# Another written-out order for the pieces of a linear-attention and channel-mix kernel

## The chip, the cores and the metric

The kernel runs on one core of a Trainium2 chip. The metric is the time of one execution on the device in microseconds (us). The core has a matrix engine (TensorE, PE in the profile, with its weight loads listed apart as PEld), a vector engine (DVE), a scalar engine (ACT), GpSimd (POOL, which here issues the loads), and SyncE (SP, which issues stores and a few copies). Each engine executes its own instructions strictly in program order and waits on semaphores for the others.

## The reference

Eight batches, eight heads of 64, 576 positions. First a linear attention without softmax, whose rows are normalised; then a channel mix in which each position is blended with the one before it.

```python
kv  = einsum('bhsd,bhse->bhde', k, v)            # per head 64 x 64
out = einsum('bhsd,bhde->bhse', q, kv)
x   = out / sqrt(mean(out*out, -1) + 1e-6) * g_norm   # -> (8, 576, 512)
x_prev = x shifted down by one position (zeros first)
xk = mu_k*x + (1-mu_k)*x_prev ;  xr = mu_r*x + (1-mu_r)*x_prev
kk = relu(xk @ w_k)                              # 512 -> 1024
v2 = (kk*kk) @ w_v                               # 1024 -> 512
y  = sigmoid(xr @ w_r) * v2                      # (8, 576, 512) float32
```

## The kernel before

Everything is kept transposed, channels on partitions, in bf16. The attention works batch by batch (b = 0 to 7); heads lie in pairs, and two pairs form a half z (0 or 1). Batches 0 and 1 are loaded and worked in halves, the others whole (the names then end in `.01`). The channel mix works in nine groups g of 512 positions, which run across batches; `xk` and `xr` are rings that hold four batches. A group needs the blended x of every batch that it touches.

The program is cut into named pieces. `Plan.add` records each with the engines it may run on, and `Plan.emit` goes through the string `ORDER` word by word and issues the instructions of each piece; `@A` or `@D` behind a name chooses ACT or DVE where both are possible. Since no scheduler comes after it, `ORDER` fixes the order on every engine's queue and on the queues of transfers. The order between engines is left to semaphores. Two readers of one PSUM tile on different engines run in the order in which they are written.

The pieces, with the line of their instructions in the profile:

| piece | engine | line | what it does |
|---|---|---|---|
| `ldh.k`, `ldh.v` | SP | L236 | fp32 load of half 0 of k, v of batch 0 into the space of `xk` |
| `cst` | ACT or DVE | L128, L130 | casts these to bf16 |
| `ld.q/k/v b`, `ld.wk/wr/wv` | POOL | L221, L226, L252 | loads with cast to bf16 |
| `seta`, `setp`, `setb`, `ident`, `perm`, `table` | DVE, POOL, ACT | L164 to L189, L144 | constants, first activation table |
| `small`, `tr9`, `cols` | SP, PE, DVE | L193, L211, L200 | mu and g as columns |
| `zz`, `z:512` | PE | L450 | matmuls of zeros, filler ahead of the first `k0` piece |
| `kv`, `kc`, `ks`, `kd` | PE, ACT or DVE, PE, ACT or DVE | L265, L128/L130, L271 | kv, copy, regrouping matmul, copy |
| `tq` | DVE | L358 | transposes q, two pieces a batch or half |
| `u` | PE | L282 | q times kv, 32-row tiles, two pieces a batch or half |
| `sq` | ACT | L379 | squares of u |
| `uc` | ACT or DVE | L134, L136 | g times u out of PSUM (not for batch 0) |
| `ss`, `rs` | PE, ACT | L408 (b 0, 1) or L388, L288 | sums of squares, reciprocal root |
| `sp` | SP | L430 | spreads `rs` over the partitions (from batch 2) |
| `mul`, `d` | DVE | L401, L405, L300 | normalised x, difference to its neighbour |
| `mk`, `mr`, `xk`, `xr` | ACT or DVE, DVE | L134, L136, L313, L320 | blends |
| `k`, `relu`, `ksq` | PE, ACT, DVE | L482, L507, L465, L493, L522 | first product, relu, square |
| `r`, `sig` | PE, ACT | L534, L544 | second product, sigmoid |
| `v`, `out`, `st` | PE, DVE, SP | L554, L567, L581, L456 | third product, gate, store |

A name's numbers are batch or group, then part: `kv2.01` is kv of batch 2, `k5.2` the third block of 128 rows of w_k in group 5, `u4.01.1` the second half of the positions of batch 4.

Loads: POOL issues them in the order of the `ld` words, each on one of eight semaphores in turn, so that the ninth waits for the first to land; a load also waits until its buffer (three each for k, v and q) is no longer read. PSUM is four tiles of two banks (`ps`), taken by kv, u, ss and the three products in the order in which they are written. `sigmoid` and the reciprocal root lie in different activation tables, so that ACT loads a table (L144) wherever a `sig` follows an `rs` or the other way round.

## Time and profile before

| what | us |
|---|---|
| three runs | 199.5, 200.09, 200.31 (median 200.09) |
| the profiled execution, its time | 200.13 |
| its span, first to last instruction | 198.4 |
| last matmul ends | 194.4 |
| first `kv` (kv0.0) starts | 7.29 |
| first `k0` piece starts | 17.01 |
| kv2.01, kv3.01, kv5.01 start | 40.67, 49.77, 58.89 |
| last load lands | 98.6 |

The table is read so: the span is what the profile sees of an execution, and 1.7 us of its time lie outside it. The granted TensorE clock is 0.997 of full speed in the mean. In the list of groups a row gives engine, operation and tile, the busy time, the mean of one instruction, and what ended the idle time before it; in a timeline a bracket gives the idle time ahead of an instruction and the releaser. "issue" as a releaser means that the profile shows no wait.

### The profile page before, as it was taken

The numbers are of one execution on the slowest core, as the hardware profiler recorded it, in microseconds if no ns is written. First come the engines' busy times: TensorE is split into PE (matmuls) and PEld (weight loads), VectorE is DVE, ScalarE is ACT, GpSimd is POOL, SyncE is SP. The second block draws the span as 40 slices with busy tenths as digits, with TensorE's granted clock in tenths as the row PEclk, the third lists the DMA queues.
The fourth block names the chain that finished last, engine by engine and source line by source line (L and its number), as shares of the span: only waits on it lengthen the run. The fifth ranks groups of instructions, "written<-read, shape, count | busy, mean of one in ns | idle before, by whom it ended". The sixth has DMA issues, their size and how long they took to land.

```text
span 198.4 us, 4225 instructions
## 1 busy us (share of the span) xinstructions
PE 188.4 (95%) x1735; PEld 93.3 (47%) x1760; DVE 137.8 (69%) x235; ACT 121.8 (61%) x158; POOL 23.7 (12%) x42
## 2 busy tenths in 40 slices
PE   7889989999999999999999999999999999999992
PEld 2445844443544544444358644444444444444451
DVE  2669998897959968998968497899659421520641
ACT  3365499949976689945778986882219840433410
POOL 7743442141313010000000000000000000000000
PEclk9999999999999999999999999999999999999998
DMA  6999999999999999999703511743213000310444
GB/s 223 191 202 214 204 201 207 214 206 216 206 235 264 216 235 272 260 240 256 210 3 88 175 72 56 220 112 78 45 47 111 2 3 0 140 71 0 153 167 160
DMA packets 21032, 30.63 MB, mean 154 GB/s; under 512 B 1932, under 2 KB 14484, under 8 KB 21012
## 3 DMA queue, kind: packets, MB, share of 16 engines
q0 software_dynamic: 11280, 16.19, 45.7%
q1 hardware_dynamic: 9588, 14.03, 22.2%
q8 instruction: 14, 0.23, 0.4%
q10 hardware_dynamic: 144, 0.13, 0.2%
q14 instruction: 6, 0.05, 0.1%
HBM read 33.56 MB, written 9.44 MB: 217 GB/s over the span
## 4 chain that ended last, share of the span: by engine, by line
PE 68%; DMA 26%; POOL 2%; issue 2%; DVE 0%; POOLq 0%
PE ps L554 27%; PE ps L507 24%; DMA v<-in_v_dram 19%; PE ps L534 12%; DMA w_v<-in_moe_w_v_dram 7%; PE ps L282 2%; PE ps L265 1%; PE ps L388 1%; POOL w_k L252 1%; POOL q L221 1%; PE ps L271 0%; POOL k L226 0%; POOL perm L189 0%; POOL v L226 0%; DVE out L581 0%
## 5 line engine op out<-in xcount | busy, mean ns | idle before, releaser
L554 PE MATMUL ps<-w_v,sqk 128*128 128x512 bf16 (+1 forms) x286 | 65.7, 373 | 0.9 <-issue 0.6
L507 PE MATMUL ps<-xk,w_k 128*128 128x512 bf16 (+1 forms) x280 | 58.1, 355 | 1.1 <-issue 0.8
L465 ACT ACTIVATE relu<-ps 128x1024 bf16<-128x1024 f32 x36 | 36.5, 1026 | 32.5 <-PE ps L507 28.8
L554 PEld LDWEIGHTS <-sqk 128*128 128x128 bf16 x296 | 27.8, 98 | 32.2 <-issue 2.5
L507 PEld LDWEIGHTS <-w_k 128*128 128x128 bf16 x288 | 27.5, 98 | 26.7 <-issue 1.4
L567 DVE TENSOR_TENSOR out<-ps,sig 128x1024 f32<-128x1024 f32 x16 | 19.4, 1221 | 21.9 <-PE ps L554 12.5
L534 PE MATMUL ps<-w_r,xr 128*128 128x512 bf16 x139 | 33.6, 379 | 0.3
L522 DVE TENSOR_TENSOR sqk<-relu 128x1024 bf16<-128x1024 bf16 x32 | 21.2, 684 | 10.0 <-ACT relu L465 9.7
L544 ACT ACTIVATE sig<-ps 128x1024 bf16<-128x1024 f32 x18 | 18.2, 1024 | 12.4 <-PE ps L534 11.5
L534 PEld LDWEIGHTS <-xr 128*128 128x128 bf16 x144 | 13.9, 98 | 16.3 <-issue 0.5
L379 ACT ACTIVATE sq<-ps 128x576 bf16<-128x576 f32 x32 | 19.9, 652 | 1.8 <-PE ps L282 1.5
L358 DVE STREAM_TRANSPOSE qT<-q 128x576 f32<-128x576 f32 (+1 forms) x20 | 14.7, 760 | 2.4 <-DMA q<-in_q_dram 2.3
L144 ACT ACT_TABLE_LOAD x12 | 15.4, 1283 | 0.9 <-PEq L607 0.7
L136 DVE TENSOR_SCALAR uT<-ps,cols 128x576 bf16<-128x576 f32 x13 | 10.4, 816 | 7.7 <-ACT sq L379 5.5
L136 DVE TENSOR_SCALAR md<-d,cols 128x576 bf16<-128x576 bf16 x44 | 13.8, 365 | 0.4
L134 ACT ACTIVATE uT<-ps,cols 128x576 bf16<-128x576 f32 x15 | 10.9, 742 | 2.9 <-PE ps L282 2.9
L300 DVE TENSOR_TENSOR d<-xT 128x1152 bf16<-128x1152 bf16 (+1 forms) x18 | 12.3, 689 | 0.4
L313 DVE TENSOR_TENSOR xr<-md,xT 128x1152 bf16<-128x1152 bf16 x14 | 10.4, 750 | 1.6 <-ACT md L134 1.4
L405 DVE TENSOR_TENSOR xT<-uT,rs 128x1152 bf16<-128x1152 bf16 x14 | 10.4, 750 | 1.1 <-ACT rs L288 0.6
L313 DVE TENSOR_TENSOR xk<-md,xT 128x1152 bf16<-128x1152 bf16 x14 | 10.4, 754 | 0.6 <-ACT md L134 0.4
L450 PE MATMUL ps<-zero 128*128 128x512 bf16 x28 | 9.4, 481 | 1.5 <-DVE zero L164 1.2
L282 PE MATMUL ps<-qT,kv 32*64 32x288 bf16 x256 | 8.5, 290 | 0.8 <-DVE qT L358 0.8
(53 smaller groups left out, 120.9 us busy)
## 6 DMA issues: line engine op xcount, KB each, us to landing
out_dram<-out SPq DMA_DIRECT2D x35, 256.0 KB, 2.3
v<-in_v_dram POOLq DMA_DIRECT2D x6, 576.0 KB, 22.9
k<-in_k_dram POOLq DMA_DIRECT2D x6, 576.0 KB, 23.2
q<-in_q_dram POOLq DMA_DIRECT2D x6, 576.0 KB, 25.5
rs<-rsc SPq DMA_DIRECT2D x48, 72.0 KB, 3.2
q<-in_q_dram POOLq DMA_DIRECT2D x4, 288.0 KB, 10.3
w_k<-in_moe_w_k_dram POOLq DMA_DIRECT2D x2, 512.0 KB, 11.4
w_v<-in_moe_w_v_dram POOLq DMA_DIRECT2D x2, 512.0 KB, 13.8
```

The costliest lines, as they stand in the source:

```text
L136: nc.vector.tensor_scalar(out=dst, in0=src, scalar1=col, scalar2=None, op0=ALU.mult)
L144: nc.scalar.preload_act_table_set(name)
L313: nc.vector.tensor_tensor(out=dst[:, 2 * z:2 * z + 2, r0:r0 + w], in0=md.t[:, :, cs], in1=xT[:, :, cur], op=ALU.add)
L358: nc.vector.transpose(out=dst[part, js], in_=src[part, js])
L379: sq_ = add("sq" + name, "A", lambda _, ps=ps, sq=sq, cs=cs, w=w: nc.scalar.activation(out=get(sq)[:, :, cs], in_=ps.t[:, :, 0:w], func=AF ...
L465: nc.scalar.activation(out=get(rt), in_=ps.t, func=AF.Relu)
L507: nc.tensor.matmul(get(ps)[:, fc % 2, a0:a1], w_k_sb[:, cc, 128 * fc:128 * fc + 128], xk[:, cc, x0:x0 + a1 - a0], start=(cc == 0), stop=(c ...
L522: nc.vector.tensor_mul(out=get(sqk)[:, 2 * f2:2 * f2 + 2, :], in0=rt.t, in1=rt.t)
L534: nc.tensor.matmul(get(ps)[:, ci % 2, :], xr[:, cc, n0:n0 + 128], w_r_sb[:, cc, :], start=(cc == 0), stop=(cc == NHP - 1))
L544: nc.scalar.activation(out=get(sg), in_=ps.t, func=AF.Sigmoid)
L554: nc.tensor.matmul(get(ps)[:, bank, cs], sqk.t[:, fc, 128 * ci:128 * ci + 128], w_v_sb[:, fc, cs], start=(fc == 0), stop=(fc == NFC - 1))
L567: dv = add(f"out{g}.{c2}", "D", lambda _, ps=ps, sg=sg, ot=ot: nc.vector.tensor_mul(out=get(ot), in0=ps.t, in1=sg.t), deps=ms + [sg_done], ...
```

## The change

Only the string `ORDER` changes. No piece is added or dropped but one `z:512` (30 words instead of 29), and no tile, size or dependency changes; what moves is the place of nearly every piece in the queues, and the engine of some copies.

- Loads: `ldh.v` goes ahead of `ldh.k` and `ident` ahead of the first load; `ld.k1.1` goes ahead of `ld.wk0`, `ld.v1.1` ahead of `ld.wk1`, `ld.k1.0` and `ld.v1.0` ahead of `ld.wr`; k and v of several batches swap, `ld.q5` and `ld.q6` and the loads of batches 6 and 7 swap.
- Engines: `kd` runs on DVE five times instead of once, `kc` once instead of twice, `cst` three times instead of twice, `uc` 14 times instead of 13; `mr` runs on ACT eight times instead of four. The words need two more table loads on ACT, 14 instead of 12.
- Startup: the pieces of batch 0 and 1 and of groups 0 and 1 are interleaved otherwise; kv0.1 goes ahead of u0.0.1, kd0.0 behind tq0.0.0.
- Middle: kv5.01, kv4.01, kv6.01 and kv7.01 stand elsewhere among the pieces of the channel mix, kv6.01 directly ahead of u5.01.0, kv7.01 ahead of u6.01.1, ss5 behind u6.01.0 and ss6 behind u7.01.0.
- End: the last piece is `v8.3.10` with its store on SP, where it was `v8.3.11` with its store on ACT.

The string is one line in the file; it is wrapped here and cut to the places that the prediction speaks of.

```diff
-ldh.k ldh.v seta setp perm ld.q0.0 ld.q0.1 ld.v0.1 ld.k0.1 ld.wk0 ident ld.wk1 ld.v1.1 ld.k1.1 ld.q1.1 ld.wr ld.q1.0 ld.v1.0 ld.k1.0 ld.wv0 ld.wv1
-ld.v2.01 ld.k2.01 ld.q2.01 table small zz cst.k0@D cst.k1@A setb cst.v0@A cst.v1@D tq0.0.1 tq0.0.0 z:512 z:512 z:512 z:512 z:512 z:512 z:512 z:512
-z:512 z:512 z:512 z:512 z:512 z:512 z:512 z:512 kv0.0 tq0.1.0 kc0.0@A z:512 z:512 ks0.0 tr9 cols kd0.0@A u0.0.0 sq0.00 z:512 z:512 z:512 ss0.00 u0.0.1
-rs0.00 mul0.00 d0.00 tq0.1.1 z:512 z:512 kv0.1 ld.k3.01 ld.v3.01 ld.q3.01 sq0.01 kc0.1@A ss0.01 rs0.01 ks0.1 kd0.1@A z:512 z:512 z:512 u0.1.0 sq0.10
-xk0.00 z:512 z:512 z:512 ss0.10 mul0.01 d0.01 xk0.01 rs0.10 mul0.10 d0.10 u0.1.1 k0.000 sq0.11 ss0.11 rs0.11 k0.110 xk0.10 k0.100 mul0.11 k0.001 d0.11
-xk0.11 relu0.00 xr0.11 xr0.00 k0.010 k0.011 kv1.1 ksq0.00 k0.111 kc1.1@A tq1.1.0 tq1.1.1 ks1.1 xr0.10 relu0.01 kd1.1@A relu0.11 ksq0.11 k0.101 xr0.01
-u1.1.1 uc1.11@A sq1.11 u1.1.0 sq1.10 uc1.10@D relu0.10 ksq0.10 r0.0 r0.1 ss1.2 ss1.3 rs1.2 rs1.3 mul1.1 kv1.0 ld.k5.01 ld.v5.01 kc1.0@D tq1.0.1
-tq1.0.0 r0.2 r0.3 sig0.0 ks1.0 kd1.0@A ksq0.01 sig0.1 v0.0.0 u1.0.1 uc1.01@D u1.0.0 v0.1.0 sq1.00 sq1.01 uc1.00@D v0.1.1 d1.1 ss1.1 rs1.1 v0.0.1
-out0.0 ss1.0 rs1.0 v0.2.0 v0.2.1 mul1.0 d1.0 mk1.0@D xk1.0 v0.3.0 v0.3.1 out0.1 mk1.1@A kv2.01
...
-u2.01.1 sq2.11 mr1.0@D k1.1.1 uc2.01@D k1.6.0 k1.7.0 k1.6.1 relu1.0 uc2.11@D u2.01.0 sq2.01 sq2.10 sq2.00 uc2.10@D k1.7.1 k1.4.0 k1.5.0 xr1.1 k1.4.1
-uc2.00@A ss2 kv3.01
...
-u3.01.0 sq3.00 v1.2.0 uc3.00@D v1.3.0 v1.2.1 sq3.10 u3.01.1 uc3.11@A uc3.10@D kv5.01 ld.k6.01 ld.v6.01 sq3.11 kc5.01@A v1.3.1 v1.1.0 ks5.01
...
-kv4.01 kc4.01@A k2.1 ks4.01 relu2.1 kd4.01@A st1.0 xr2.0 mr2.1@D xr2.1 ksq2.1 relu2.0 tq4.01.0 tq4.01.1 ld.q7.01 k2.4 k2.5 relu2.2 k2.6 r2.2 r2.3
-u4.01.0
...
-kv6.01 out3.0 kc6.01@A st2.3 xk4.0 xr4.0 ss5 rs5 sp5.0 v3.3.1 out3.1 ks6.01 st3.1 k4.6 kd6.01@A k4.7 relu4.3 u6.01.0
...
-kv7.01 mr5.1@A ss6 v4.2.0 mk5.0@D xk5.0 xk5.1 kc7.01@A ks7.01 out4.0 kd7.01@D st4.0 v4.2.1 xr5.1 rs6 sp6.1 u7.01.1 uc7.01@A uc7.11@A v4.3.1 sq7.11
-out4.1 st4.3 st2.0 st4.2 sq7.01 k5.2 k5.3
...
-rs7 v5.1.0 v5.2.0 v5.2.1 r5.2 v5.3.0 mk6.0@D mr6.1@D xk6.0 xr6.1 mr6.0@D r5.0 xr6.0 r5.1 sig5.0 r5.3 sig5.1 xk6.1 v5.0.0 sp7.1 v5.0.1 mul7.1 v5.3.1
-out5.1 r6.0 r6.1 k6.4
...
-v8.0.00 v8.1.10 sig8.0 st7.0 v8.2.00 v8.2.10 out8.10 st8.10 sig8.1 out8.20 st8.20 v8.0.10 out8.00 v8.3.00 v8.3.10 out8.30 st8.00 st8.30 v8.3.01
-v8.3.11 out8.31 st8.31
...
+ldh.v ldh.k seta table setp perm ident ld.q0.0 ld.q0.1 ld.v0.1 ld.k0.1 ld.k1.1 ld.wk0 ld.v1.1 ld.wk1 ld.q1.1 ld.k1.0 ld.v1.0 ld.wr ld.q1.0 ld.wv0
+ld.wv1 ld.k2.01 ld.v2.01 ld.q2.01 small zz cst.v0@D cst.v1@D cst.k0@A setb cst.k1@D tq0.0.1 z:512 z:512 z:512 z:512 z:512 z:512 z:512 z:512 z:512
+z:512 z:512 z:512 z:512 z:512 z:512 z:512 kv0.0 kc0.0@A z:512 z:512 ks0.0 tq0.0.0 kd0.0@D tq0.1.1 z:512 z:512 u0.0.0 tr9 tq0.1.0 sq0.00 cols z:512
+ss0.00 rs0.00 mul0.00 d0.00 xk0.00 z:512 z:512 z:512 kv0.1 ld.v3.01 ld.k3.01 ld.q3.01 kc0.1@A u0.0.1 z:512 ks0.1 sq0.01 kd0.1@D z:512 ss0.01 rs0.01
+mul0.01 d0.01 xk0.01 z:512 z:512 u0.1.0 sq0.10 u0.1.1 sq0.11 z:512 z:512 ss0.10 rs0.10 mul0.10 d0.10 xk0.10 k0.000 ss0.11 rs0.11 mul0.11 xr0.10 d0.11
+tq1.1.0 k0.010 tq1.1.1 kv1.1 k0.001 xk0.11 kc1.1@A ks1.1 kd1.1@A relu0.00 ksq0.00 k0.011 relu0.01 k0.110 u1.1.1 u1.1.0 k0.100 uc1.11@A sq1.11 sq1.10
+k0.111 k0.101 xr0.00 relu0.11 uc1.10@D ss1.3 kv1.0 ld.k5.01 ld.v5.01 rs1.3 ss1.2 relu0.10 r0.0 xr0.01 xr0.11 kc1.0@A ksq0.11 tq1.0.1 r0.2 r0.3 ks1.0
+rs1.2 tq1.0.0 mul1.1 kd1.0@D sig0.1 r0.1 ksq0.10 u1.0.0 ksq0.01 uc1.00@D sig0.0 u1.0.1 sq1.01 v0.2.0 v0.3.0 uc1.01@D sq1.00 d1.1 mk1.1@D v0.1.0 ss1.1
+ss1.0 rs1.1 rs1.0 v0.0.0 v0.0.1 v0.3.1 v0.1.1 v0.2.1 xk1.1 kv2.01
...
+tq2.01.0 tq2.01.1 ld.q5.01 k1.1.0 k1.0.1 u2.01.1 k1.1.1 relu1.1 k1.6.0 k1.7.0 k1.6.1 sq2.11 uc2.01@D relu1.0 uc2.11@D u2.01.0 sq2.01 k1.4.0 ksq1.0
+k1.5.0 xr1.0 k1.4.1 sq2.00 k1.5.1 uc2.00@D mr1.1@D ksq1.1 xr1.1 sq2.10 ss2 uc2.10@A kv3.01
...
+u3.01.0 sig1.1 v1.1.1 v1.0.0 sp2.0 uc3.10@A uc3.00@D sq3.00 sq3.10 u3.01.1 v1.2.0 v1.2.1 mul2.1 d2.1 mk2.1@D xk2.1 v1.3.0 sq3.01 uc3.01@A kv5.01
+ld.v7.01 ld.k7.01 st0.0 sq3.11 uc3.11@A ss3 v1.0.1 mul2.0 d2.0 mk2.0@D rs3 sp3.0 xk2.0 kc5.01@A v1.3.1 out1.0 ks5.01
...
+kv4.01 relu2.2 ksq2.0 v2.2.0 xr2.0 tq4.01.0 ksq2.2 k2.6 tq4.01.1 ld.q7.01 kc4.01@A ks4.01 sp3.1 xr2.1 k2.7 kd4.01@A relu2.3 v2.3.0 ksq2.3 u4.01.1
...
+kv6.01 sig3.0 d4.0 mr4.0@D kc6.01@A u5.01.0
...
+u6.01.0 uc6.00@D sig3.1 ss5 rs5 sq6.00 v3.2.1 st3.0 st2.1 v3.3.1 xr4.0 k4.2 out3.1 k4.3
...
+kv7.01 sig4.0 st3.3 sq6.10 sp5.0 kc7.01@A u6.01.1
...
+u7.01.0 uc7.00@D ss6 uc7.10@A mk5.0@D xk5.1 sq7.10 sq7.00 v4.3.0 v4.3.1 st3.2 mr5.0@D r4.2 r4.3 xk5.0 xr5.0 rs6 sig4.1 out4.1 sp6.0 k5.2 st4.2 k5.3
+k5.0 k5.1 relu5.0 ksq5.0 k5.4 k5.5 relu5.1 ksq5.1 relu5.2 k5.6 xr5.1 u7.01.1 sq7.01 ksq5.2 k5.7
...
+rs7 d6.0 r5.2 mul6.1 d6.1 mr6.1@D mr6.0@A mk6.0@D v5.3.0 v5.3.1 mk6.1@D xr6.0 r5.3 xk6.0 sig5.1 v5.1.0 xk6.1 k6.6
...
+v8.2.00 v8.1.00 v8.3.01 v8.1.10 v8.0.00 v8.0.10 out8.10 st8.10 v8.2.10 st6.1 out8.00 v8.3.00 st8.00 out8.20 v8.3.11 out8.31 st8.31 v8.3.10 st8.20
+out8.30 st8.30
...
```

## The prediction

> **What bounds the kernel now.** I read the page first: busy shares, slices, then the chain that ended last.
>
> ```profile
> span 198.4 us, 4225 instructions
> ...
> PE 188.4 (95%) x1735; PEld 93.3 (47%) x1760; DVE 137.8 (69%) x235; ACT 121.8 (61%) x158; POOL 23.7 (12%) x42
> ...
> DMA  6999999999999999999703511743213000310444
> ...
> PE 68%; DMA 26%; POOL 2%; issue 2%; DVE 0%; POOLq 0%
> ```
>
> TensorE (PE) is full, 188.4 of 198.4 us, and neither DVE nor ACT has a share of the chain. The transfers are busy for half the span. The chain in order of time says where each of the two sets the end:
>
> ```profile
> 6.54 12.88 DMA v<-in_v_dram
> ...
> 19.70 14.54 DMA w_v<-in_moe_w_v_dram
> ...
> 34.52 24.23 DMA v<-in_v_dram
> ...
> 58.89 0.77 PE ps L265 x72
> ```
>
> Three hops of loads carry it to 58.76 (34.52 + 24.23); from there it is PE alone. Each hop is a wait of one load for an earlier one: the loads issued by POOL land one behind the other. Issue plus time to landing of single loads gives v2 37.1, k2 40.6, q2 43.4, v3 49.0 and v5 58.76, about 2.8 us for a full k, v or q of 576 KB, 1.4 us for a half, 2.5 us for a weight. PE's timeline and that of its weight loads show which landings hurt:
>
> ```profile
> 58.89 0.77 PE L265 MATMUL ps<-v,k 64*64 64x64 bf16 x72 [0.35 <-DMA v<-in_v_dram]
> ...
> 40.67 0.67 PEld L265 LDWEIGHTS <-k 64*64 64x64 bf16 x72 [0.46 <-DMA k<-in_k_dram]
> ...
> 44.95 0.18 PEld L282 LDWEIGHTS <-kv 32*64 32x64 bf16 x16 [0.65 <-issue]
> ...
> 49.41 0.12 PEld L388 LDWEIGHTS <-heads 128*32 128x32 bf16 x8 [0.42 <-DVE uT L136]
> 49.77 0.67 PEld L265 LDWEIGHTS <-k 64*64 64x64 bf16 x72 [0.24 <-issue]
> ...
> 67.29 0.67 PEld L265 LDWEIGHTS <-k 64*64 64x64 bf16 x72 [0.42 <-issue]
> ...
> 73.51 0.16 PEld L282 LDWEIGHTS <-kv 32*64 32x64 bf16 x16 [0.42 <-issue]
> ```
>
> kv5.01 waits 0.35 for v5; kv2.01 starts at 40.67, just as k2 has landed. The third kind of row matters too: a weight load of a small-tile piece (kv, u, the 8-matmul ss) that follows a piece of k, r or v comes after 0.42 us of idle, where weight loads of the big pieces are 0.11 apart. So each entry from big tiles into small ones costs about 0.30. kv3.01 right behind ss2 has 0.24, which is ss2's own matmuls: that entry was free.
>
> The startup is set by DVE, which the timeline shows busy without a gap from 12.22 to 28.3:
>
> ```profile
> 8.34 2.24 DVE L358 STREAM_TRANSPOSE qT<-q 64x576 f32<-64x576 f32 x3 [1.54 <-DMA q<-in_q_dram]
> ...
> 12.22 0.82 DVE L401 SCALAR_TENSOR_TENSOR xT<-ps,cols,rs 128x576 bf16<-128x576 f32 x1 [1.41 <-ACT rs L288]
> ...
> 13.57 0.78 DVE L358 STREAM_TRANSPOSE qT<-q 64x576 f32<-64x576 f32 x1
> ```
>
> The sum below is against this execution: 200.13 us, of which 198.4 is its span; the median is 200.09, so the two agree.
>
> **The change, part by part.** No tile, size or dependency changes; PE has the same pieces and one more zero matmul (0.22 warm, in a stretch where PE waits for DVE anyway: 0).
>
> *Startup to kv2.01.* The same 18 loads are queued ahead of k3/v3, so v2 and k2 together still land at about 40.6. In between, k1.1 goes ahead of both w_k halves and w_r behind k1.0 and v1.0. With the intervals above, w_k0 lands at 16.7 (15.2 before), w_k1 at 20.7 (18.3), k1.0 and v1.0 by 25 (29.2), w_r 27.5 (24.8), q1.0 28.9 (26.2). What that does to PE: k0.000 is reached at about 17, so w_k0 is hidden by 0.3; k0.001 waits some 0.6 for w_k1 and xk0.10; the wait of 0.82 that kv1.0 had for k1.0 (ss1.3 issued at 28.50, kv1.0 at 29.56, its own work 0.24) goes.
> DVE: kd0.0 moves from ACT onto DVE behind both transposes of q0.0: these end at 9.77 and kd adds 0.41, so u0.0.0 runs at 10.35 instead of 9.82. With the same 2.4 us through sq, ss and rs, mul0.00 starts at 12.75 (12.22). tq0.1.1 no longer stands between d0.00 and xk0.00 (-0.78), but kd0.1 does behind it (+0.41), and u0.0.1 now follows kv0.1 (k0.1 lands at 12.7) so that rs0.01 ends near 15.95: mul0.01 at 16.0 (15.24). From there each of the groups mul, d, xk takes 2.27 as before, with xr0.10 (0.95) and the two tq1.1 (1.5) ahead of xk0.11. tq1.1.1 ends at 24.2, which releases u1.1.1. PE goes on from there; DVE then has 8.3 us of pieces up to kd1.0 (xk0.11, ksq0.00, three xr, uc1.10, ksq0.11, two tq1.0, mul1.1, kd1.0 by the rows of L320, L493, L136, L358, L405, L130), so u1.0.0 runs at 32.65 and v0.2.0 at 33.3. From v0.2.0 to kv2.01 stand 7.4 us of PE pieces and 0.25 of entries: 40.95 against 40.67. **+0.3.** Bounds: -0.75 if k2 lands a usual 2.8 behind v2 (it took 3.55 here) and the startup loses nothing; +1.5 if the 0.74 of mul0.01, kd1.0's 0.41 and a later q0.0 (ident now ahead of it on POOL, 0.19) all reach kv2.01. I take the walk, being nearest to the rows.
>
> *u2.01.1.* It issued 0.53 late, 0.2 more than an entry, because the transposes of q2 (landed 43.4) ended at 44.84. PE comes 0.3 later, so this goes: **-0.2** (0 to -0.2).
>
> *kv5.01.* It has 41.35 us of PE pieces since k0.000 ahead of it instead of 38.76. With the start at 17 and 2.5 us of entries and waits it is reached near 60.8, and v5, still the 23rd load, lands near 58.8. The wait goes: **-0.35** (0 to -0.39). kv4 (49.56 us of pieces, 3 of entries) is reached near 69.5; k4 and v4 are still the 24th and 25th load and land by 66.5. What is late next is kv3, reached at 49.9 with k3 at 49.0.
>
> *Entries.* Counted over both orders from k0.000 on, big-to-small entries fall from 20 to 18 (u 12 to 10, ss 4 to 3, kv 4 to 5): **-0.6**, if the new neighbours (kv6 then u5, kv7 then u6, u6 then ss5, u7 then ss6) are free, as kv3 behind ss2 was (0.24 against 0.24). Bounds: -0.6, and +0.6 if these four pay 0.30 each. The page TensorE: Matmul & The Clock Gate of the Trainium skill (Part 2, the step on LDWEIGHTS) says that a weight load is pulled ahead of running matmuls only where the row groups don't conflict or the background weight buffer takes it; kv uses 64 rows and u 32, so by that rule the two kv-to-u neighbours would pay 0.30 each, and the sum would be 0.6 higher. The row that is there, ss2 then kv3, uses overlapping row groups and paid nothing; no row shows kv then u.
>
> *Middle, where DVE's cover gets thin.* k5.2 needs xk5.0. Before, xk5 was done at 120.70 and k5.2 issued at 123.97. Now uc7.00, mk5.0, xk5.1, mr5.0 and xk5.0 stand on DVE between u7.01.0 and k5.2: 0.74 + 4 x 0.68 to 0.76, 3.6 us with the semaphores, against ss6 and four big pieces on PE, 0.36 + 4 x 0.865 = 3.8. u6.01.1 needs the PSUM of sq6.10, which now stands behind sig4.0 on ACT, within 0.2 of PE's arrival. **+0.3** for both (0 to +0.9). The groups of k3, k4, k6 and k8 keep 0.7 to 1.9 by the same walk.
>
> *ACT and queues.* Two more table loads (14 for 12, 1.283 each) and four mr pieces moved from DVE to ACT (1.44 each) (DVE's total stays near 138: four kd, a cast and a uc come, four mr and a kc go) lie where ACT idles (121.8 busy of 198.4; a wait of 3.49 before sig5.0 at 138.29): 0, up to +0.5 through out4.1, behind the table load for sig4.1, which frees PSUM 0.9 us ahead of k5.6. On SP, sp and st swap places; spreads are needed 3 us or more after their rs and land in 3.2: 0.
>
> *Tail.* The last store goes to SP instead of ACT: 194.01 to 195.80 there against 194.89 to 196.65, 1.79 against 1.76: 0.
>
> Sum: 0.3 - 0.2 - 0.35 - 0.6 + 0.3 = -0.55, so 200.13 - 0.55 = **199.6**. A measurement of this kernel tells about 0.5%, 1.0 us, from no change; this lies inside it.
>
> **Rivals.** *Faster.* Loads set kv2.01 and the startup costs nothing: kv2.01 at 40.0, the other terms without the +0.3: 200.13 - 0.7 - 0.2 - 0.35 - 0.6 = 198.3. For it: kv1.0's 0.82 goes, 3.55 for k2 is out of line. Against: DVE has no idle time to catch up from 12.75 to 33.
> *Slower.* DVE's startup chain decides: the 0.74 lag at mul0.01 plus every piece put ahead of xk0.11 and kd1.0 reaches kv2.01. With kv2.01 at 43.2 (+2.5) the sum is 200.13 + 2.5 - 1.15 + 0.3 = 201.8. It decides from kv2.01 at 42.5 on (+1.85, the point at which the total passes +1.0). For it: u1.1.1 and u1.0.0 have no slack in my walk. Against: even 0.5 more at each leaves 42.0.
> *The change does nothing measurable on another ground.* The FIFO of loads sets kv2 and kv3 as before, the new neighbours pay 0.30 each: 199.6 + 1.2 = 200.8, inside 0.5% too. Speaking for it, four entries of the kind are in every other place 0.30; against it, kv3 behind ss2.
>
> **How the numbers follow.** My sum 0.35 (199.6) and the third rival 0.16 (200.8) make 0.51 within 0.5%; faster 0.22 (198.3), slower 0.27 (201.8): thin covers can only add. The range goes from the faster rival, 198.3, to a little over the slower one, 202.1; each end leaves out about a tenth.
>
> **What would show it.** kv2.01 (first x72 of L265) at 40.9, u0.0.0 at 10.35, mul0.00 at 12.75; no DMA wait ahead of L265 after 45 us; 0.24 or less, not 0.42, of idle ahead of the u loads behind kv6 and kv7; no gap at k5.2. Wrong if kv2.01 is past 42, if a gap over 0.5 us stands ahead of a k piece (DVE) or a u piece (PSUM held by ACT) after 80 us, or if loads land otherwise than in queue order at these intervals.

## The result and the profile after

The changed kernel takes 200.84 us (median of 22 runs, 200.05 to 201.63) against 199.86 for the kernel before on the same chip (22 runs, 199.25 to 200.62): a ratio of 1.0046, with a 95% interval of 1.0032 to 1.006. So it is about 0.9 us slower, just inside the 0.5% that the prediction called no change, where the prediction had it 0.5 us faster. The profiled execution took 200.80 us, in the middle of its runs; that of before took 200.13, above its median.

The head of the page, its slices and the shares of the chain, of the changed kernel:

```profile
span 198.9 us, 4254 instructions
...
PE 191.1 (96%) x1761; PEld 93.6 (47%) x1761; DVE 136.5 (69%) x232; ACT 127.7 (64%) x163; POOL 23.7 (12%) x42
...
DMA  6999999999999999999355102451602002110263
...
PE 81%; DMA 7%; DVE 5%; SPq 2%; POOL 1%; issue 1%; ACT 1%; DVEq 0%; POOLq 0%
```

Busy times hardly differ. The chain does: its DMA share falls from 26% to 7%, PE's rises from 68% to 81%, and DVE, which had 0%, has 5%. The hops of loads no longer carry the end; TensorE and DVE do. Now the weight loads of TensorE in order of time (start, duration, idle before, and what ended it):

```profile
19.81 0.64 PEld L265 LDWEIGHTS <-k 64*64 64x64 bf16 x36 [0.21 <-issue]
21.02 0.77 PEld L482 LDWEIGHTS <-w_k 128*128 128x128 bf16 x8 [0.56 <-DMA w_k<-in_moe_w_k_dram]
...
40.83 0.67 PEld L265 LDWEIGHTS <-k 64*64 64x64 bf16 x72 [0.42 <-issue]
...
44.89 0.16 PEld L282 LDWEIGHTS <-kv 32*64 32x64 bf16 x16 [0.42 <-issue]
...
60.85 0.67 PEld L265 LDWEIGHTS <-k 64*64 64x64 bf16 x72 [0.42 <-issue]
...
64.53 1.41 PEld L507 LDWEIGHTS <-w_k 128*128 128x128 bf16 x8 [0.66 <-DVE xk L313]
```

In this execution kv2.01 (40.83), u2.01.1 (44.89) and kv5.01 (60.85) are as predicted, without a wait for data. k2.2 at 64.53 waits 0.66 for DVE; before, it came without a wait:

```profile
64.39 2.47 PEld L507 LDWEIGHTS <-w_k 128*128 128x128 bf16 x12
```

TensorE's last weight load ends at 193.98, against 194.11 before. And yet the span is 0.5 longer, so in this pair the loss is behind TensorE's last piece. DVE's last rows, after:

```profile
187.38 1.22 DVE L567 TENSOR_TENSOR out<-ps,sig 128x1024 f32<-128x1024 f32 x1 [0.84 <-PE ps L554]
190.40 0.69 DVE L581 TENSOR_TENSOR out<-ps,sig 128x512 f32<-128x512 f32 x1 [1.80 <-PE ps L554]
192.13 0.69 DVE L581 TENSOR_TENSOR out<-ps,sig 128x512 f32<-128x512 f32 x1 [1.03 <-PE ps L554]
193.84 1.35 DVE L581 TENSOR_TENSOR out<-ps,sig 128x512 f32<-128x512 f32 x3 [1.02 <-PE ps L554]
```

and before:

```profile
191.88 1.50 DVE L581 TENSOR_TENSOR out<-ps,sig 128x512 f32<-128x512 f32 x2 [1.03 <-PE ps L554]
193.56 0.42 DVE L581 TENSOR_TENSOR out<-ps,sig 128x256 f32<-128x256 f32 x1 [0.18 <-PE ps L554]
194.43 0.42 DVE L581 TENSOR_TENSOR out<-ps,sig 128x256 f32<-128x256 f32 x1 [0.45 <-PE ps L554]
```

After, out8.20 (193.84) runs 1.38 us behind the last weight load of v8.2.10, before 0.59; the profile names PE, but v8.2.10 had been done at 192.97. It waited for two stores: DVE passed its waits on the semaphores of st7.3 and st7.2 at 193.12 and 193.75. The three last outs then run back to back, their stores bunch up, and the last lands at 197.38 (2.16 after issue) instead of 196.65 (1.76 after issue).

### The profile page after: what moved, and what is told of

Its sections match the earlier page's. It is cut to its first block, busy times and chain, and to the rows that moved or that the text cites. A ratio compares the mean times of both kernels' runs of the same rounds, so it can differ in the third digit from the quotient of the medians.

```text
span 198.9 us, 4254 instructions
## 1 busy us (share of the span) xinstructions
PE 191.1 (96%) x1761; PEld 93.6 (47%) x1761; DVE 136.5 (69%) x232; ACT 127.7 (64%) x163; POOL 23.7 (12%) x42
## 4 chain that ended last, share of the span: by engine, by line
PE 81%; DMA 7%; DVE 5%; SPq 2%; POOL 1%; issue 1%; ACT 1%; DVEq 0%; POOLq 0%
PE ps L554 28%; PE ps L507 28%; PE ps L534 14%; DMA k<-in_k_dram 4%; PE ps L482 3%; PE ps L282 3%; DMA rs<-rsc 3%; SPq L430 2%; PE ps L265 2%; DVE xT L401 1%; PE ps L271 1%; DVE xk L320 1%; PE ps L388 1%; DVE d L300 1%; PE ps L408 1%
## 5 line engine op out<-in xcount | busy, mean ns | idle before, releaser
L554 PE MATMUL ps<-w_v,sqk 128*128 128x512 bf16 (+1 forms) x296 | 67.0, 374 | 0.0
L507 PE MATMUL ps<-xk,w_k 128*128 128x512 bf16 (+1 forms) x288 | 58.8, 356 | 0.5 <-DVE xk L313 0.5
L534 PE MATMUL ps<-w_r,xr 128*128 128x512 bf16 x144 | 34.9, 379 | 0.0
L134 ACT ACTIVATE md<-d,cols 128x576 bf16<-128x576 bf16 x20 | 14.3, 772 | 1.6 <-DVE d L300 1.6
L136 DVE TENSOR_SCALAR uT<-ps,cols 128x576 bf16<-128x576 f32 x14 | 11.2, 814 | 3.0 <-PE ps L282 2.0
L450 PE MATMUL ps<-zero 128*128 128x512 bf16 x31 | 11.1, 493 | 1.2 <-DVE zero L164 1.2
L136 DVE TENSOR_SCALAR md<-d,cols 128x576 bf16<-128x576 bf16 x36 | 11.5, 365 | 0.4
L134 ACT ACTIVATE uT<-ps,cols 128x576 bf16<-128x576 f32 x14 | 10.3, 743 | 1.2 <-PE ps L282 1.2
```

Source lines behind the costliest of these rows:

```text
L134: nc.scalar.mul(out=dst, in_=src, mul=col)
L136: nc.vector.tensor_scalar(out=dst, in0=src, scalar1=col, scalar2=None, op0=ALU.mult)
L507: nc.tensor.matmul(get(ps)[:, fc % 2, a0:a1], w_k_sb[:, cc, 128 * fc:128 * fc + 128], xk[:, cc, x0:x0 + a1 - a0], start=(cc == 0), stop=(c ...
L534: nc.tensor.matmul(get(ps)[:, ci % 2, :], xr[:, cc, n0:n0 + 128], w_r_sb[:, cc, :], start=(cc == 0), stop=(cc == NHP - 1))
L554: nc.tensor.matmul(get(ps)[:, bank, cs], sqk.t[:, fc, 128 * ci:128 * ci + 128], w_v_sb[:, fc, cs], start=(fc == 0), stop=(fc == NFC - 1))
```

## The experiments

**How the loss is counted.** For each piece of TensorE from k0.000 on: the start of its first weight load less the summed durations of all pieces ahead of it (0.865 for a big piece, 0.71 for kv, 0.38 for u and so on). It is counted from 17.01 in every profile, the start of k0.000 in that of before; k0.000 starts at 16.3 to 17.7 in the others, which is part of the first stage. Both orders have the same sum, 172.30 us, up to the last piece, so the differences by stage add up. Three theories came from the first pair of profiles: A, the loss is the wait of out8.20; B, it is the wait of k2.2; C, it is in startup and loads.

**A fourth out buffer.**

```diff
-        "out": (3, (128, 2, C), FP32),
+        "out": (4, (128, 2, C), FP32),
```

> The changed kernel with four out buffers instead of three, nothing else. In its trace out8.20 (L581) could have started at 192.97, when v8.2.10 was done, and started at 193.84, because it takes the buffer of out7.1 and the stores st7.3 and st7.2 landed at 193.09 and 193.72. Theory A (the loss lies in this wait): out8.20 follows its matmuls, the two last outs are no longer queued behind it, and the last store, no longer bunched with the two before it (2.16 us from issue to landing, against 1.76 before), lands near 196.5 instead of 197.38: about 199.95, and a ratio to before of about 1.000. Theory B (the loss lies in the wait of 0.66 of k2.2 for xk2.0 at 64 us): nothing changes here, 200.8 and 1.0045. Theory C (the loss is spread over the startup and the loads): 200.8 too.

Measured: 200.43, ratio 1.0036 (1.0022 to 1.0049). out8.20 starts 0.59 behind v8.2.10's last weight load, and the last store lands at 196.72. The mechanism is as A says, but less than half of the loss goes.

**st6.1 earlier.** Its late place makes out8.10 take the buffer of out7.0 and out8.20 that of out7.1.

```diff
-st6.0 k8.6 ... v8.2.10 st6.1 out8.00
+st6.0 st6.1 k8.6 ... v8.2.10 out8.00
```

> The changed kernel with st6.1 issued right behind st6.0 instead of behind v8.2.10. Then the buffer of out6.0 is free before out8.10 takes one: out8.10 gets it, and out8.20 gets that of out7.0, whose stores landed by 186.2. Theory A: as with a fourth buffer, about 199.95 and a ratio of 1.000, with one store (256 KB, 16 engines) less in the last 7 us, so perhaps 0.1 less again. Theories B and C: 200.8, ratio 1.0045.

Measured: 200.78, ratio 1.0048 (1.0029 to 1.0068), no gain that six runs can tell. Its trace says why that is no contradiction: out8.20 waits for nothing, the span ends 4.16 behind the last weight load (4.96 in the changed kernel), but this execution lost 2.33 us up to kv2.01, the first one 1.74. That made C worth its own runs.

**The two halves of batch 2 swapped.**

```diff
-sp2.1 ... sp2.0 ... mul2.1 d2.1 mk2.1@D xk2.1 ... mul2.0 d2.0 mk2.0@D ... xk2.0 ... k2.2
+sp2.0 ... sp2.1 ... mul2.0 d2.0 mk2.0@D xk2.0 ... mul2.1 d2.1 mk2.1@D ... xk2.1 ... k2.2
```

> The changed kernel with the two halves of batch 2 swapped behind ss2: the spread, product, difference, mix and xk of z 0 first, those of z 1 second, as before has the spreads. k2.2 needs z 0 for its first two matmuls and z 1 for the last two. Theory B: its wait of 0.66 falls to about 0.25 (xk2.1 done at 64.5 and needed at 64.3), so 0.4 less: 200.4, ratio 1.0025. Theory A: the same at k2.2, and the tail as it was (out8.20 waits for the stores of out7.1, which move with it). If something behind k2.2 was waiting anyway, 200.8.

Measured: 200.71, ratio 1.0045 (1.0025 to 1.0066); the profiled execution took 199.79. In it k2.2 issues without the wait, and between kv5.01 and kv4.01 TensorE loses 0.38 instead of 0.76. The trace gives B its 0.4; alone, these times do not show it. The chain of the changed kernel tells where the wait came from:

```profile
49.49 0.39 PE ps L388 x8
...
49.90 0.75 ACT rsc L288
...
50.66 0.68 SPq L430
...
55.92 5.33 DMA rs<-rsc
...
61.46 0.76 DVE xT L405
62.22 0.02 issue
62.24 0.77 DVE d L300
...
63.72 0.77 DVE xk L313
...
64.54 1.47 PE ps L507 x6
```

From ss2 to k2.2 it takes 15.05 us: the root, eight spread issues one behind the other on SP (50.66 to 55.88), 5.33 for the last of them to land among the loads, then mul, d, mk and xk of the second half. TensorE has 14.4 us in between, its usual gaps included. As both ends move with ss2, the wait comes back in all seven profiles that keep this order of the halves (0.66 to 0.90), and no lateness ahead of ss2 is absorbed by it.

**Control: before with four out buffers.**

> The kernel before with four out buffers: a control. In its trace no out waits for a store at the end, so by every theory it is 199.9 and the ratio 1.000 (within 0.001). A change of more would say that addresses or the numbering of the store queues matter by themselves.

Measured: 199.97, ratio 1.0014 (1.0001 to 1.0027). A fourth buffer alone brings nothing, if anything a loss of 0.3.

**Each startup with the other's rest.**

```diff
-ldh.v ldh.k seta table ... v0.1.1 v0.2.1 xk1.1 kv2.01 ld.k4.01 ...
+ldh.k ldh.v seta setp ... v0.3.1 out0.1 mk1.1@A kv2.01 xk1.1 ld.k4.01 ...
```

> The order of before up to and with kv2.01, the changed order behind it (both have done the same pieces there but for xk1.1, mul1.0, d1.0, mk1.0, xk1.0 and two outs). Theory C, formed on the four profiles of the changed startup so far: TensorE stops at k0.001 until w_k1, there the eighth load, has landed (20.92, 20.98, 21.16 and 21.56 in four executions; k0.001 starts 0.04 to 0.1 behind each), and all that follows to kv2.01 is a string without slack, so kv2.01 comes at 40.8 to 41.4 against 40.4 to 40.7 with the startup of before. Its share of the loss is then about 0.4, and this kernel takes about 200.4, ratio 1.0025. Theory A (the loss is all in the wait of out8.20 at the end): 200.8. Theory B (k2.2's wait): 200.8.

```diff
-ldh.k ldh.v seta setp ... v0.3.1 out0.1 mk1.1@A kv2.01 ld.v4.01 ...
+ldh.v ldh.k seta table ... v0.1.1 v0.2.1 xk1.1 kv2.01 mul1.0 d1.0 mk1.0@D xk1.0 out0.1 out0.0 ld.v4.01 ...
```

> The mirror of it: the changed order up to and with kv2.01, the order of before behind it. Theory C: kv2.01 0.2 to 0.7 later than in before; behind it, before has a wait of up to 0.39 for v5 at kv5.01, which takes up as much of that: 199.9 to 200.3, ratio 1.000 to 1.002. Theories A and B: the tail and k2.2 are those of before, 199.85, ratio 1.000.

Measured: before's startup and the changed rest 200.36, ratio 1.0031 (1.0002 to 1.0061); the changed startup and before's rest 199.96, ratio 0.9999 (0.9977 to 1.0021). So these runs tell no cost of the changed startup if before's rest follows. The traces show the reason. In before's order kv5.01 starts 0.10 us behind the landing of v5 in the four profiles of before's order, in one of them with a load moved and in one with four out buffers: 58.86 (v5 at 58.76), 58.93 (58.83), 58.02 (57.91), 58.63 (58.52). A later start only shortens that wait: with the changed startup and before's rest it came at 58.30, and v5 had landed at 57.84:

```profile
58.30 0.66 PEld L265 LDWEIGHTS <-k 64*64 64x64 bf16 x72 [0.23 <-issue]
```

In the changed order hardly a load is awaited behind kv2.01 (only kv3.01 in the run with four out buffers, by 0.1), and what is lost at the start is lost at the end: in the five profiles of the changed startup and rest that keep the order of batch 2's halves and of the loads, kv2.01 comes at 40.79 to 41.71, and TensorE's last weight load always ends 153.15 to 153.38 behind it. With before's rest that distance goes from 152.74 to 153.69.

**All three suspects taken away**: the edits of before's startup, of the swap and of the fourth buffer in one kernel.

> The changed order with the three suspects taken away together: the startup of before up to kv2.01 (theory C, 0.4), z 0 of batch 2 ahead of z 1 (theory B, 0.4), four out buffers (theory A, 0.4 by the times of that run). If the three add up, 200.84 - 1.2 = 199.6, ratio 0.9985, what the prediction gave for the change without them. If there is a fourth cause, it stays above 200.

Measured: 200.11, ratio 1.0000 (0.9975 to 1.0024). Against before the loss is gone, so there is no fourth cause of a size that these runs tell. But the sum of 1.2 was too much, and the 0.5 which the prediction saw as a gain does not appear either.

**w_k1 one place earlier.**

```diff
-ld.wk0 ld.v1.1 ld.wk1 ld.q1.1 ... k0.010 tq1.1.1 kv1.1 k0.001 ... ks1.1 ... k0.011 relu0.01 k0.110
+ld.wk0 ld.wk1 ld.v1.1 ld.q1.1 ... k0.010 tq1.1.1 k0.001 ... k0.011 kv1.1 ... k0.110 ks1.1 ... relu0.01
```

> The changed kernel with one load moved, ld.wk1 ahead of ld.v1.1, and kv1.1 (which needs v1.1) with its copies behind k0.011 in the order. Theory C: w_k1 lands near 19.1, k0.001 goes as soon as xk0.10 is done (20.3 instead of 21.0 to 21.6), and tq1.1.1 at 23.7 is the next limit, for u1.1.1: 0.4 to 0.9 less at u1.1.1 (23.8 instead of 24.2 to 24.8) and at kv2.01, 200.3, ratio 1.002. Theories A and B: 200.8.

Measured: 200.88, ratio 1.0058 (1.0028 to 1.0088): theory C in this form fails. Weight loads of this run:

```profile
20.10 1.62 PEld L482 LDWEIGHTS <-w_k 128*128 128x128 bf16 x15 [0.19 <-issue]
...
24.46 0.39 PEld L282 LDWEIGHTS <-kv 32*64 32x64 bf16 x16 [0.62 <-ACT kv L128]
```

The wait for w_k1 is gone (k0.001 at 19.81), and kv1.1, now behind four k0 pieces, passes its lateness on to kd1.1 on ACT and so to u1.1.1. kv2.01 ends up with a loss of 2.43, no better than the 1.70 to 2.72 of the changed order. w_k1 was the last to arrive, not the only one without slack.

**Both kernels again.**

> The kernel before, unchanged, for a second profile of it. The prediction took 0.2 at u2.01.1 and 0.35 at kv5.01 as gains, because the one profiled execution of before, 200.13 and so 0.27 above the median of 22 runs, waited there. In the profile with four out buffers (199.81) TensorE loses 0.90 over the summed durations of its pieces between kv2.01 and kv5.01, in the one profile of before 1.51. Theory D (these waits belong to one execution): 0.9 again, and kv5.01 without a DMA wait. Else: 1.5, and the wait of 0.35 for v5.

> The changed kernel, unchanged, for a second profile of it and more times: ratio 1.0046 as before. k2.2 waits for the second product chain of batch 2 by 0.65 to 0.9 (theory B, in all profiles of this order so far), out8.20 by 0.1 to 0.8 for the last lane of the stores of out7.1 (theory A), and kv2.01 comes at w_k1's landing plus 19.8 (theory C).

Measured: before 199.76, ratio 1.0001 (0.9987 to 1.0016); the changed kernel 201.10, ratio 1.0069 (1.0049 to 1.009, 6 runs), its profiled execution 201.22. Theory D holds in half: the second profile of before has a gap of 0.36 at kv5.01 and loses 1.13 between kv2.01 and kv5.01 (1.51 and 0.90 in the two others), since it came to kv2.01 later. In that of the changed kernel:

```profile
21.90 0.77 PEld L482 LDWEIGHTS <-w_k 128*128 128x128 bf16 x8 [1.77 <-DMA w_k<-in_moe_w_k_dram]
...
65.57 0.33 PEld L507 LDWEIGHTS <-w_k 128*128 128x128 bf16 x3 [0.82 <-DVE xk L313]
```

k0.001 waits 1.77 for w_k1 and k2.2 0.82; out8.20 only 0.18.

**The changed startup with both later waits gone** (the swap of batch 2 and four out buffers).

> The changed kernel with its own startup, z 0 of batch 2 ahead of z 1, and four out buffers. If the waits of k2.2 (about 0.4 of it net, since kv4.01 then waits 0.1 to 0.25 for its loads) and of out8.20 (0.4 on average) are separate and both lie on the path: 200.85 - 0.8 = 200.05, ratio 1.001, and what is left, 0.2, is the startup. If only one of them counts: 200.45, ratio 1.003.

Measured: 200.15, ratio 1.0014 (0.9999 to 1.0029), 0.95 less than the changed kernel beside it (0.7 less than in the first measurement), though its profiled execution lost 2.72 at kv2.01. So the two waits together hold most of the loss. The expectation misread one thing: the small rest at kv4.01 is no load; it is the third matmul of k2.2 waiting for xk2.1:

```profile
64.81 0.37 PEld L507 LDWEIGHTS <-w_k 128*128 128x128 bf16 x3
65.70 4.41 PEld L507 LDWEIGHTS <-w_k 128*128 128x128 bf16 x21 [0.52 <-issue]
```

**k1.0 earlier in before, alone and with the changed rest.**

```diff
-ld.wr ld.q1.0 ld.v1.0 ld.k1.0
+ld.wr ld.v1.0 ld.k1.0 ld.q1.0
```

> The kernel before with one load moved: ld.q1.0 behind ld.v1.0 and ld.k1.0 (the changed order has these two ahead of it as well). kv1.0 waits 0.8 for k1.0 in all four profiles of the startup of before; k1.0 then lands 1.4 earlier and the wait goes. Theory E (kv2.01 is held by PE's own string in the startup): kv2.01 0.3 to 0.7 earlier, 199.4, ratio 0.998. Theory F (the loads hold kv2.01 and what follows: k2 landed at 39.9 to 40.6, v2 and q2 beside it): no change, 199.85, ratio 1.000.

> The startup of b_k10 (before's order up to kv2.01, with ld.q1.0 behind ld.v1.0 and ld.k1.0), the changed order behind it with z 0 of batch 2 first, and four out buffers. With the startup of before this was 200.1. Theory E (TensorE's string in the startup sets kv2.01, and nothing behind it takes up the difference in this order, which no longer waits for v5): kv2.01 0.3 to 0.6 earlier, 199.7, ratio 0.999. Theory F (loads hold kv2.01 in any case): 200.1, ratio 1.000 to 1.001.

Measured: alone 199.83, ratio 1.0003 (0.9991 to 1.0014); with the changed rest 200.18, ratio 1.001 (0.9991 to 1.0029). In the first k1.0 landed at 27.78 instead of 28.8 to 30.0, and kv2.01 then waited for k2 (40.36, landed 40.30), kv5.01 for v5 (58.63, landed 58.52). That is theory F. In the second kv2.01 came with a loss of 1.58, within what the startup of before has without this edit, so E found no support. No version beat before.

**out7.1 and its stores earlier.**

```diff
-v7.2.0 v7.2.1 sig7.0 r8.2 ... st7.1 v7.3.0 v7.3.1 out7.1 st7.3 st7.2 v8.2.00
+v7.2.0 v7.2.1 sig7.0 v7.3.0 v7.3.1 out7.1 st7.3 st7.2 r8.2 ... st7.1 v8.2.00
```

> The changed kernel with v7.3.0, v7.3.1, out7.1, st7.3 and st7.2 ahead of r8.2 instead of behind r8.3; out buffers stay three and st6.1 where it is. out8.20 then takes the buffer of out7.0, whose stores are issued near 187 and land by 189.5. Theory G (the late lane is the one that carries the 16 KB of the instruction queue near 190.7, and the stores in flight then wait behind it): no lane of the stores of out7.0 and out7.1 is late, out8.20 follows v8.2.10 without a wait, the end of the span comes 4.2 us behind the last weight load instead of 4.3 to 5.0, and the time is about 0.35 less than the changed kernel's, ratio to before 1.003. If the lane is late for another reason (the two stores of one out back to back), it is late here too, by about 2 us.

Measured: 200.75, ratio 1.0034 (1.0018 to 1.005), near the 1.003 expected, but the interval takes in the changed kernel's 1.0046 too, so that the trace has to tell. In it the first of the three last outs follows its matmuls again:

```profile
193.97 1.68 DVE L581 TENSOR_TENSOR out<-ps,sig 128x512 f32<-128x512 f32 x3 [0.23 <-PE ps L554]
```

The span ends 4.16 behind the last weight load. No lane of the five stores issued from 186.09 to 188.21 is more than 0.05 behind the 15 others. In the ten profiles that keep the changed tail (the one with st6.1 moved among them) the sixteenth lane of st7.2 comes 1.7 to 2.4 us late. So the lateness is not a property of two stores back to back; what fits is the 16 KB transfer on the instruction queue, at 190.50 in this run.

## Why the prediction was wrong, point by point

The loss by stages, in us, means over the profiles that leave the stage as it is in the one order or the other (three of before, five to seven of the changed order, three for its tail), beside the terms of the sum. The kernels with a load moved and those joined from two orders are left out.

| stage | before | changed | difference | the prediction |
|---|---|---|---|---|
| k0.000 to kv2.01 | 1.65 (1.35 to 2.03) | 2.21 (1.70 to 2.72) | +0.56 | +0.3 |
| kv2.01 to kv5.01 | 1.18 (0.90 to 1.51) | 0.77 (0.75 to 0.85) | -0.41 | -0.2 - 0.35 |
| kv5.01 to kv4.01 | 0.42 (0.22 to 0.60) | 0.89 (0.76 to 0.99) | +0.47 | 0 |
| kv4.01 to the last piece | 1.09 | 1.00 | -0.09 | -0.6 + 0.3 |
| last weight load to the end of the span | 4.23 | 4.51 (4.23 to 4.96) | +0.28 | 0 |
| sum | | | +0.81 | -0.55 |

The sum comes near the 0.9 to 1.4 of the times. Few profiles stand behind each mean, so the shares are good to some 0.2: with the joined kernels counted too, the startup loses 1.76 with before's order (five profiles) and 2.18 with the changed one (eight), which is +0.41 instead of +0.56.

*Startup.* DVE's timeline of the changed kernel, with kd0.0 (9.69) behind both transposes and mul0.00 at 12.53:

```profile
8.33 1.43 DVE L358 STREAM_TRANSPOSE qT<-q 64x576 f32<-64x576 f32 x2 [1.25 <-DMA q<-in_q_dram]
9.69 0.38 DVE L130 CAST kv<-ps 64x256 bf16<-64x256 f32 x1
...
12.53 0.82 DVE L401 SCALAR_TENSOR_TENSOR xT<-ps,cols,rs 128x576 bf16<-128x576 f32 x1 [0.73 <-ACT rs L288]
```

In the first pair the steps on TensorE and DVE came close to what was written: u0.0.0 at 10.12 (10.35 predicted), mul0.00 at 12.53 (12.75), v0.2.0 at 33.33 (33.3), kv2.01 at 40.83 (40.95). The size was that of a good execution: over more of them the term is +0.4 to +0.56. The step that fell short is "k0.001 waits some 0.6 for w_k1": the waits were 0.44 to 1.77 (w_k1 at 20.93 to 21.96, predicted 20.7). In all eight profiles with this startup k0.001 starts within 0.05 of w_k1's landing, and kv2.01 comes 19.81 or 19.82 behind k0.001. So it is this load that sets kv2.01 here, and not DVE's startup chain, as the slower rival had it; the run with w_k1 earlier shows only that other pieces stand close behind it.

*u2.01.1 and kv5.01.* Both waits went, as the sum had it. But a wait for a load is no cost that an order can simply save: it takes up what was lost ahead of it. The startup's +0.56 and this -0.41 are one term of +0.15, where the sum had -0.25, read off an execution that stood 0.27 above the median.

*Entries.* The largest term, -0.6, was sized by half of its rows. The weight loads of u5.01.0 between two big pieces before, and of kv6.01 with u5.01.0 behind it after:

```profile
97.36 0.96 PEld L554 LDWEIGHTS <-sqk 128*128 128x128 bf16 x5
98.74 0.15 PEld L282 LDWEIGHTS <-kv 32*64 32x64 bf16 x16 [0.42 <-issue]
99.12 1.19 PEld L554 LDWEIGHTS <-sqk 128*128 128x128 bf16 x7 [0.23 <-issue]
```

```profile
94.37 0.67 PEld L265 LDWEIGHTS <-k 64*64 64x64 bf16 x72 [0.42 <-issue]
95.07 0.15 PEld L282 LDWEIGHTS <-kv 32*64 32x64 bf16 x16
95.45 0.98 PEld L554 LDWEIGHTS <-sqk 128*128 128x128 bf16 x6 [0.23 <-issue]
```

The entry is 0.31 late. But the big piece behind it gives 0.20 back: its four weight loads take 0.66 instead of 0.86 until the next piece. An entry and its exit cost 0.11 together. From kv4.01 on two entries less saved 0.06 in the first pair and 0.09 in the means. That the new neighbours are free was right: u follows kv with 0.04 between their weight loads. So the 0.30 that the prediction drew from the rule on row groups (the Trainium skill, TensorE: Matmul & The Clock Gate, Part 2) does not appear for kv ahead of u; the rule itself is not against that, since it lets a load also go ahead into the background weight buffer.

*Thin covers.* The 0.3 for k5.2 and u6.01.1 did not occur; k5.2 shows no gap. The loss from kv4.01 on is 1.00 in every profile of the changed order.

*"On SP, sp and st swap places; spreads are needed 3 us or more after their rs and land in 3.2: 0."* This step failed: it took the median of all spreads for those of batch 2. The median is 3.7 now, but those of batch 2 land among the loads, 5.33 for the last, behind eight issues of 0.6. The trace of before had this already: there the eight spreads of batch 2 take 5.5 to 6.2 from issue to landing. In before the same chain ends as late (xk2.1 at 64.84), but only the second pair of k2.2's matmuls needs that. The changed order runs the half needed first as the second.

*Tail, put at 0.* This step failed too. It priced the last store by its time from issue to landing, and not by the buffer that the last outs take: with the new places of st6.1 and out7.1, out8.20 gets a buffer whose stores are still under way. The price is between 0.08 and 0.79 in the five profiles that keep it; without it the tail is 4.15 to 4.30 in six, about that of before (4.22 to 4.25).

The rival called slower named the right sign with a mechanism that was not there: it needed kv2.01 at 42.5 or later, and 41.81 was the latest. The third rival named 200.8, almost the time that was measured, but that is luck: it had the four new neighbours pay 0.30 each, and none does (0.04 of idle ahead of u behind kv, 0.23 ahead of ss behind u, as for kv3 behind ss2). And the prediction's sign of being wrong, a gap over 0.5 ahead of a k piece, watched only the time after 80 us; the gap stood at 64.5.

## What to carry to other kernels

Take a wait for a load out of the sum only together with all that runs ahead of it, for it absorbs lateness, and an order without such waits passes every late landing on to its end. Price a change of neighbours from a piece that is surely undisturbed to the next such one: the gap ahead of a piece may be given back behind it. And when stores move, follow the ring of their buffers to the last user; when halves swap, ask which of them the next consumer reads first.

## What the runs showed that was not expected

The trace has sixteen landings for each transfer, called lanes here, and a wait ends with the last of them. In the tail and at w_k1 one lane of the sixteen is late. In the profiled execution of the changed kernel 15 landings of st7.2 are in by 191.31, 2.30 us after issue, and the sixteenth at 193.72. That lane then works off its share of five stores, 0.60 to 0.65 us apart, until 195.58. What fits in place and time is a transfer of the instruction queue, of which the view of the DMA queues from 186 to 198 us shows one:

```profile
q8 instruction: 1, 0.02, 0.5%
```

It is a packet of 16 KB that starts at 190.67 and takes 0.93, less than the 2.4 by which the lane is late, so how the one delays the other stays open. The same stands elsewhere in both orders: beside 16 KB packets at 109.56 before and 109.79 after, the spreads issued at 108.26 and 107.97 have a last lane 1.62 and 1.75 late. A like packet starts at 15.7 to 16.7 in every startup, and v1.1 and w_k1, the loads that follow, have a last lane up to 1.8 us late: 15 lanes of w_k1 land by 20.09 to 20.92, near the 20.7 predicted, and the last at 20.93 to 21.96. For the tail, moving the stores ahead of the packet took the late lane away, as in before, where st7.2 and st7.3 are issued at 185.2 to 186.3 and no lane is more than 0.03 late; for the startup the link is only argued. The Trainium skill (DMA: Bandwidth & Descriptors, the section on why a DMA increments its semaphore by 16) says that each of the engines of one transfer adds its own count when its part is done and only the full count means landed. The trace agrees: DVE went on 0.12 us after the sixteenth landing of st7.2 and not 2.4 earlier.
